# A linear-attention and snake-MLP kernel: the unused matmuls of its head made 512 columns wide

## The chip, the cores and the metric

The kernel runs on one core of one Trainium2 chip. The metric is the device time of one execution in microseconds (us). Three runs of the kernel before are shown, and a fourth execution was recorded by the hardware profiler.

## The reference, cut to what matters

Two layers follow each other. The first is causal linear attention with a decay per head, over 4 batches, 8 heads, 768 positions and a head width of 64. The second is a wide layer on the 3072 tokens by 512 features that come out.

```python
# attention, per block of 64 positions
intra = (qb @ kb.T * Dmask) @ vb
inter = (qb * lam_pow) @ kv_state
out[:, :, sl] = intra + inter
kv_state = lam_block * kv_state + (kb * rev_pow).T @ vb
# wide layer: 512 -> 2048 -> 512
h = x @ w_in
s = np.sin(alpha * h)
g = h + s * s / (alpha + 1e-09)
return g @ w_out
```

## The kernel before, in words

**Tiles.** Attention works on 24 blocks of 128 tokens. For each, q and k are scaled by powers of the decay (DVE or GpSimd, L462 to L492), transposed so that the head width lies on partitions (TensorE, L534, L560 and L511 for most of the early blocks, a DMA for the rest), and multiplied to scores (L612). DVE multiplies the scores by a mask (L623). Scores times v (L759, L716) and queries times the running state (L779, L694, L707) give the output of the block, which is copied to `xT`. The state itself is k times v, summed in PSUM (L648, L656) and copied to `Zd` or `Zc`. The wide layer takes chunks of 512 tokens. `unit_A` and `unit_A2` (L822, L856) make one or two slices of 128 hidden features: four matmuls each, then a sine on ScalarE, a square on ScalarE or GpSimd, and the sum on DVE. `unit_B` (L887) and `unit_P` (L975) make the second product.

**Head.** The first four blocks are loaded together. SyncE issues in this order: the decays, q in two halves, four loads of k, four loads of v, two loads `ws` of the first quarter of `w_in` (cast to `w1` by DVE at L384). GpSimd issues the loads of the other quarters of `w1` and of `w2` behind its casts of v (L486); ScalarE casts one of the four loads of v, in its own order ahead of the copies of the state (L666). TensorE's first state product (L648) needs two casts of v, both from GpSimd.

**Order.** No scheduler decides the order. `_Plan.ORDER` lists for each engine the numbers of its operations in the order in which it issues them; a semaphore wait is put where an operation depends on another engine. An engine issues strictly in this order, so an operation that waits holds back all behind it. In TensorE's list a pair like `(42,112)` isn't an operation. It is 42 unused matmuls of 112 columns, made by `spin` from a constant tile `idle` (which is part of `Xs`, set to 1.0 by DVE at L410) into PSUM bank 0. Their result is overwritten. They depend on nothing but `idle`, and nothing waits for them; they are recorded under L1134. Each has its own weight load, which is an instruction of its own.

TensorE's list begins as follows, with the meaning of the numbers:

```text
(42,112)  39: transpose of alpha (L444)
(30,128)  57: transposes of q (L534)    (11,128)  55: L534   (1,128)  53: L534   (1,128)  59: L534
(8,128)   61: transposes of k (L560)    (1,512)   62: L560
(3,512)   65, 67: scores (L612)   69, 70: L560   (3,512)  73: L612
75: first state product (L648)    78: L612   80: L759   82: L648   85: L779   (2,512)   87: L648
```

Of the kernel before, what the change touches and what calls it, by code (L numbers as in the profile page):

```python
# [33 lines left out]
class _Plan:  # L34

    ORDER = {
        "PE": (
            (42,112), 39, (30,128), 57, (11,128), 55, (1,128), 53, (1,128), 59, (8,128), 61, (1,512), 62,
            (3,512), 65, 67, 69, 70, (3,512), 73, 75, 78, 80, 82, 85, (2,512), 87, 90, 91, 93, 124, 130, 140,
            136, 151, 155, 147, 144, 167, 163, 159, 230, 228, 175, 171, 229, 232, 231, 233, 183, 191, 187, 179,  # L40
            235, 206, 207, 234, 209, 236, 217, 215, 237, 241, 221, 245, 319, 226, 320, 249, 250, 272, 252, 258,
# [1204 lines left out]
```

## Time and profile before

| What | us |
|---|---|
| median of three runs | 210.94 (210.78 to 211.43) |
| profiled execution, its own time | 211.5 |
| span in its trace, first to last instruction | 209.8 |
| TensorE busy in the span | 203.5 |
| DVE, ScalarE, GpSimd busy | 160.3, 158.7, 126.9 |

The span is shorter than the profiled execution's own time by 1.7 us, which lie around it. In the lines of the profile PE is TensorE's matmuls, PEld its weight loads, DVE is VectorE, ACT is ScalarE, POOL is GpSimd and SP is SyncE; a q behind an engine's name (SPq) is its sequencer, issuing a DMA. L534 is line 534 of the kernel. A line of a list in order of time has the start, the length and what ran, with xN for N instructions merged; brackets hold the idle time before it and what ended that. Matmuls overlap, so the length of a group ends with the tail of its last matmul. A row of a table of stretches has the stretch, its length, then for PE, PEld, DVE, ACT and POOL the busy time and the number of instructions, then the granted clock, the busy share of the DMA engines and GB/s. A row of a DMA queue has packets, MB and the share of 16 engines' time; a row of DMA issues ends with the time from issue to landing.

### The profile page before, as it was taken

The numbers are of one execution on the slowest core, as the hardware profiler recorded it, in microseconds if no ns is written. First come the engines' busy times: TensorE is split into PE (matmuls) and PEld (weight loads), VectorE is DVE, ScalarE is ACT, GpSimd is POOL, SyncE is SP. The second block draws the span as 40 slices with busy tenths as digits, with TensorE's granted clock in tenths as the row PEclk, the third lists the DMA queues.
The fourth block names the chain that finished last, engine by engine and source line by source line (L and its number), as shares of the span: only waits on it lengthen the run. The fifth ranks groups of instructions, "written<-read, shape, count | busy, mean of one in ns | idle before, by whom it ended". The sixth has DMA issues, their size and how long they took to land.

```text
span 209.8 us, 4867 instructions
## 1 busy us (share of the span) xinstructions
PE 203.5 (97%) x1975; PEld 134.3 (64%) x1975; DVE 160.3 (76%) x266; ACT 158.7 (76%) x294; POOL 126.9 (60%) x130
## 2 busy tenths in 40 slices
PE   7979999999999999999998999999999999999995
PEld 6847444457677776555555667766667765666894
DVE  4884557563999866868899799889698699777643
ACT  4949995968998989999997887787963889568210
POOL 7075354994469578679885392944581957378300
DMA  4999999999998999999999920190000004000514
GB/s 141 310 318 232 206 213 237 246 229 256 220 264 205 227 245 230 223 233 196 246 271 228 213 53 0 33 271 2 3 0 3 0 23 179 3 0 0 200 40 163
DMA packets 78998, 33.35 MB, mean 159 GB/s; under 512 B 55408, under 2 KB 76160, under 8 KB 78976
## 3 DMA queue, kind: packets, MB, share of 16 engines
q1 hardware_dynamic: 73744, 27.14, 56.2%
q0 software_dynamic: 3696, 3.67, 10.5%
q10 hardware_dynamic: 1536, 2.24, 3.3%
q8 instruction: 15, 0.25, 0.5%
q14 instruction: 7, 0.06, 0.1%
HBM read 27.28 MB, written 6.29 MB: 160 GB/s over the span
## 4 chain that ended last, share of the span: by engine, by line
PE 83%; DVE 6%; DMA 3%; SPq 3%; ACT 2%; issue 1%
PE bank L822 27%; PE bank L975 22%; PE bank L887 13%; PE bank L856 10%; DMA v<-in_v_dram 3%; PE bank L716 3%; SPq L315 3%; PE bank L612 3%; DVE gT L839 2%; PE bank L694 1%; DVE Sm L623 1%; PE bank L511 1%; PE bank L656 1%; DVE w L930 1%; PE bank L534 1%; PE bank L707 1%
## 5 line engine op out<-in xcount | busy, mean ns | idle before, releaser
L822 PE MATMUL bank<-xT,w 128*128 128x512 bf16 x296 | 70.5, 379 | 0.0
L839 DVE SCALAR_TENSOR_TENSOR gT<-u,rinv,bank 128x512 bf16<-128x512 bf16 x74 | 53.6, 742 | 18.2 <-ACT u L836 12.5
L832 ACT ACTIVATE t<-bank,alpha 128x512 bf16<-128x512 f32 x74 | 50.0, 684 | 21.0 <-PE bank L822 20.5
L822 PEld LDWEIGHTS bank<-xT,w 128*128 128x128 bf16 x296 | 28.3, 98 | 28.4 <-DVE gT L839 0.4
L836 ACT ACTIVATE u<-t 128x512 bf16<-128x512 bf16 x59 | 36.5, 628 | 1.3
L837 POOL TENSOR_TENSOR u<-t 128x512 bf16<-128x512 bf16 x15 | 16.0, 1066 | 34.1 <-ACT t L832 30.5
L953 POOL TENSOR_TENSOR gT<-gT 128x512 bf16<-128x512 bf16 x24 | 27.8, 1172 | 11.2 <-DVE Xs L953 6.0
L623 DVE TENSOR_TENSOR Sm<-bank,mask 128x1024 bf16<-128x1024 f32 x24 | 29.1, 1218 | 4.3 <-PE bank L648 1.8
L887 PE MATMUL bank<-w,gT 128*128 128x512 bf16 x128 | 31.4, 380 | 0.0
L874 DVE SCALAR_TENSOR_TENSOR gT<-u,rinv,bank 128x256 bf16<-128x256 bf16 x44 | 18.8, 476 | 7.8 <-ACT u L870 6.1
L472 POOL TENSOR_TENSOR qk<-q,Lq 128x512 bf16<-128x512 f32 x20 | 21.2, 1075 | 2.8 <-DMA q<-in_q_dram 2.8
L856 PE MATMUL bank<-xT,w 128*128 128x256 bf16 x176 | 22.2, 273 | 0.0
L492 POOL TENSOR_TENSOR qk<-k,Lk 128x512 bf16<-128x512 f32 x20 | 20.9, 1053 | 0.6 <-DMA k<-in_k_dram 0.6
L866 ACT ACTIVATE t<-bank,alpha 128x256 bf16<-128x256 f32 x44 | 18.9, 476 | 2.0 <-PE bank L856 1.5
L887 PEld LDWEIGHTS bank<-w,gT 128*128 128x128 bf16 x128 | 11.7, 98 | 12.2
L856 PEld LDWEIGHTS bank<-xT,w 128*128 128x128 bf16 x176 | 16.4, 98 | 3.5 <-issue 0.3
L953 POOL TENSOR_TENSOR Xs<-gT 128x512 bf16<-128x512 bf16 x13 | 16.1, 1235 | 1.5 <-DVE gT L839 1.4
L975 PE MATMUL bank<-w,gT 128*128 128x256 bf16 (+1 forms) x136 | 16.3, 266 | 0.0
L975 PE MATMUL bank<-w,Xs 128*128 128x256 bf16 (+1 forms) x136 | 16.0, 267 | 0.1
L975 PE MATMUL bank<-ws,gT 128*128 128x256 bf16 x128 | 15.8, 273 | 0.0
L975 PEld LDWEIGHTS bank<-w,gT 128*128 128x128 bf16 x136 | 12.6, 98 | 3.2
L975 PEld LDWEIGHTS bank<-w,Xs 128*128 128x128 bf16 x136 | 12.4, 98 | 2.8 <-DVE osb L1021 0.3
(101 smaller groups left out, 276.0 us busy)
## 6 DMA issues: line engine op xcount, KB each, us to landing
q<-in_q_dram SPq DMA_DIRECT2D x12, 512.0 KB, 6.2
k<-in_k_dram SPq DMA_DIRECT2D x24, 256.0 KB, 5.5
v<-in_v_dram SPq DMA_DIRECT2D x24, 256.0 KB, 5.4
out_dram<-osb SPq DMA_DIRECT2D x14, 256.0 KB, 2.5
w<-in_moe_w_out_dram POOLq DMA_DIRECT2D x4, 512.0 KB, 11.4
w<-in_moe_w_in_dram POOLq DMA_DIRECT2D x3, 512.0 KB, 9.0
ws<-in_moe_w_in_dram SPq DMA_DIRECT2D x2, 512.0 KB, 7.5
out_dram<-osb ACTq DMA_DIRECT2D x8, 128.0 KB, 4.0
```

What stands on the lines that cost most here:

```text
L472: lambda e, a=a: e.tensor_tensor(qk2[:, j:j + 2, 4 * a:4 * a + 4, :], q32[:, jq, 4 * a:4 * a + 4, :, :].rearrange("p h t d -> p t h d"), b ...
L492: lambda e: e.tensor_tensor(qk2[:, j, H:2 * H, :], block32(k32, jl), lk, ALU.mult), 1.05,
L623: op("DVE", lambda e: e.tensor_tensor(Sm[js][:, :, :], banks[:, 512 * b0:512 * b0 + 1024].rearrange("p (c i) -> p c i", i=128), bass.AP(ma ...
L822: ins = e.matmul(ps[hb][:, c0:c1], w1[:, kc, 128 * m:128 * (m + 1)], xT[x][:, kc, c0:c1], start=(kc == 0 and c0 == lo), stop=(kc == NKC - ...
L832: op("ACT", lambda e: e.activation(t16[ju][:, w], ps[hb][:, w], ACTF.Sin, scale=alpha[:, m:m + 1]), 0.69 if hi - lo == TCH else 0.475, [ba ...
L836: lambda e: (e.activation(u16[ju][:, w], t16[ju][:, w], ACTF.Square) if e is nc.scalar else e.tensor_tensor(u16[ju][:, w], t16[ju][:, w], ...
L839: op("DVE", lambda e: e.scalar_tensor_tensor(out=gT[g][:, m, w], in0=u16[ju][:, w], scalar=rinv[:, m:m + 1], in1=ps[hb][:, w], op0=ALU.mul ...
L856: ins = e.matmul(ps[hb][:, 256 * i:256 * i + 256], w1[:, kc, 128 * (m + i):128 * (m + i + 1)], xT[x][:, kc, lo:lo + 256], start=(kc == 0 a ...
L866: op("ACT", lambda e, i=i: e.activation(t16[ju][:, 256 * i:256 * i + 256], ps[hb][:, 256 * i:256 * i + 256], ACTF.Sin, scale=alpha[:, m + ...
L887: ins = e.matmul(ps[ob][:, w], gT[g][:, m, 128 * s4:128 * (s4 + 1)], w2[:, m, w], start=(m == 0), stop=(m == NM - 1),)
L953: e.tensor_tensor(dst, in0, in1, alu), 0, rd, wr))
L975: ins = e.matmul(ps[ob][:, lo + d0:lo + d1], lhs, rhs[:, d0:d1], start=first and p == 0, stop=(p == NM // 2 - 1), skip_group_check=True)
```

## The change

The first six pairs of TensorE's list are changed. Up to operation 61, the unused matmuls are all 512 columns wide; the two single ones between 55, 53 and 59 are gone. The pairs after 61 stay as they were. Counted up to 61, there were 93 unused matmuls and are 21. Nothing else differs, and the other engines issue the same instructions in the same order.

```diff
     ORDER = {
         "PE": (
-            (42,112), 39, (30,128), 57, (11,128), 55, (1,128), 53, (1,128), 59, (8,128), 61, (1,512), 62,
+            (9,512), 39, (7,512), 57, (3,512), 55, 53, 59, (2,512), 61, (1,512), 62,
             (3,512), 65, 67, 69, 70, (3,512), 73, 75, 78, 80, 82, 85, (2,512), 87, 90, 91, 93, 124, 130, 140,
```

## The prediction

> **What bounds the kernel now.** I read the page first, for the engine that sets the end.
>
> ```profile
> span 209.8 us, 4867 instructions
> ...
> PE 203.5 (97%) x1975; PEld 134.3 (64%) x1975; DVE 160.3 (76%) x266; ACT 158.7 (76%) x294; POOL 126.9 (60%) x130
> ...
> q8 instruction: 15, 0.25, 0.5%
> ...
> PE 83%; DVE 6%; DMA 3%; SPq 3%; ACT 2%; issue 1%
> ```
>
> TensorE is busy 97% of the span and holds 83% of the chain that ended last. So a shift of the moment when its dense work begins reaches the end. What the chain holds besides TensorE lies partly in the head, so the second view is the chain of waits cut to the first 20 us (start, length, what).
>
> ```profile
> 4.14 1.43 SPq L315
> ...
> 5.61 1.17 SPq L315
> ...
> 6.82 0.76 SPq L315
> ...
> 7.63 6.83 DMA v<-in_v_dram
> 14.46 0.02 issue
> 14.49 0.62 ACT v L486
> 15.11 0.27 ACT Zd L666
> ```
>
> Until 14.46 us the chain is not on TensorE at all. It is SyncE handing out loads, then the third load of v, then ScalarE's cast of it. The third view is TensorE's own order of time (start, length of the group, count; in brackets the idle time before it and what ended it).
>
> ```profile
> 1.52 3.55 PE L1134 MATMUL bank<-Xs 128*128 128x112 bf16 x42 [1.52 <-DVE Xs L410]
> 5.00 0.23 PE L444 MATMUL bank<-identf,alphaT 16*128 16x16 f32 x1
> 5.16 1.85 PE L1134 MATMUL bank<-Xs 128*128 128x128 bf16 x30
> 7.20 0.40 PE L534 MATMUL bank<-ident,qk 128*128 128x128 bf16 x4 [0.18 <-DVE qk L462]
> 7.43 0.78 PE L1134 MATMUL bank<-Xs 128*128 128x128 bf16 x11
> ...
> 9.74 0.39 PE L560 MATMUL bank<-ident,qk 128*128 128x128 bf16 x4
> 9.97 0.81 PE L1134 MATMUL bank<-Xs 128*128 128x512 bf16 x3
> 10.80 0.64 PE L612 MATMUL bank<-qkT 64*64 64x128 bf16 x32
> ...
> 12.96 0.42 PE L612 MATMUL bank<-qkT 64*64 64x128 bf16 x16
> 14.29 0.62 PE L648 MATMUL bank<-v,qk 64*128 64x128 bf16 x8 [0.90 <-POOL v L486]
> ```
>
> The unused matmuls (L1134) fill the time up to real work. At 14.29 TensorE has stood idle 0.90 us for GpSimd's cast of v. Whatever happened before that is forgotten there, as long as TensorE is less than 0.90 us late.
>
> **Why v is late.** The loads of k and v are alike (256 KB), so their landings should be evenly spaced. Here are four answers on DMA, each for the window in which one issue starts (last k, then v's first three; the last number is us from issue to landing), and one on the queues between 10.45 and 11.70 us.
>
> ```profile
> k<-in_k_dram SPq DMA_DIRECT2D x1, 256.0 KB, 6.4
> ```
> ```profile
> v<-in_v_dram SPq DMA_DIRECT2D x1, 256.0 KB, 5.8
> ```
> ```profile
> v<-in_v_dram SPq DMA_DIRECT2D x1, 256.0 KB, 6.7
> ```
> ```profile
> v<-in_v_dram SPq DMA_DIRECT2D x1, 256.0 KB, 6.8
> ```
> ```profile
> q8 instruction: 1, 0.02, 5.9%
> ```
>
> With the issue times of the chain (4.14, 5.61, 6.82, 7.63) the landings are 10.5, 11.4, 13.5 and 14.4 us: steps of 0.9, then 2.1, then 0.9. About 1.2 us were lost once, between the first and the second v. In that very stretch the instruction queue q8 read one packet of 0.02 MB, and it took 5.9% of 16 engines' 1.25 us, that is 1.18 us of one engine. A load has landed only when every engine has delivered its part. One engine held for 1.2 us therefore explains the step: all later loads on it stay late.
>
> Whose instructions are these? q8 read 15 packets, 0.25 MB; TensorE ran 1975 matmuls and as many weight loads, which is 263 of its instructions and 17 KB to a packet, 63 bytes each. No other engine has so many. The row of the stretches counts TensorE's instructions before the first read.
>
> ```profile
> 0.00:10.45 10.45, 8.74 (x122) 8.07 (x122) 6.69 (x17) 7.39 (x16) 3.88 (x16) 1.00 0.83 225
> 10.45:17.65 7.20, 5.91 (x138) 3.72 (x137) 5.89 (x7) 4.44 (x10) 5.64 (x8) 1.00 1.18 306
> ```
>
> The first read comes after 244 instructions. The second comes 275 later: the same q8 row answers for 17.65 to 18.90 us, and none for the time between. That is roughly every 256, by place in the program and not by time.
>
> [...]
>
> **The change part by part.**
>
> *Columns.* Up to the first transposes of q (L534) the fill goes from 42 x 112 + 30 x 128 = 8544 columns to 9 x 512 + 7 x 512 = 8192.
>
> ```profile
> L1134 PE MATMUL bank<-Xs 128*128 128x112 bf16 x24 | 2.4, 301 | 0.0
> ```
> ```profile
> 1.68 2.63 PE L1134 MATMUL bank<-Xs 128*128 128x112 bf16 x26
> ```
> ```profile
> 4.42 0.65 PE L1134 MATMUL bank<-Xs 128*128 128x112 bf16 x10
> ```
>
> The first 26 start (2.63 - 0.30) / 25 = 93 ns apart, 0.83 ns a column. The ten from 4.42 on take 0.65 us, with some 0.2 of tail 49 ns apiece. So the array runs at half rate until about 4.3 us and fully after, though the page shows a granted clock of 1.00 throughout. At full rate three 512-wide ones take 0.81 us and nine in the dense part 2.11 (row below): six more in 1.30, 216 ns each. A cold 512-wide one isn't in this trace: by columns 512 x 0.83 = 427 ns; at least 216 (full rate), at most about 635 (427 plus the 0.21 us by which 301 exceeds 93, if nothing overlapped). I take 427, the same stream. The first block then holds 2.78 us / 0.83 = 3340 cold columns; the rest is 1270 columns at 0.42 ns where it was 1360 in pieces of 112 at 49 ns: 0.53 in place of 0.60 us. The second takes 7 x 0.216 = 1.51 us against 30 x 0.056 = 1.68. TensorE waits 0.25 us longer for the transposes at 7.20, which DVE releases. Behind them 3 x 216 = 0.65 us stand for 11 x 56 = 0.61 (+0.03), the two single ones go, 2 x 216 stand for 8 x 56 (-0.02). The transposes at 9.74 and the scores at 10.80 come 0.07 us earlier. By itself this is worth nothing: the 0.90 us wait covers it. With 635 ns the first block would end at 5.4 to 5.6, and the wait at 7.20 still covers that.
>
> *Instructions.* 93 unused matmuls become 21: 72 matmuls with 72 weight loads go, 144 instructions. The first read now comes 144 instructions further on. Behind 10.45 us stand 32 + 8 + 3 + 16 + 8 = 67 matmuls up to the end of L648; 72 reaches five into the third group of scores. These wait for the second mask product on DVE:
>
> ```profile
> 11.27 3.49 DVE L623 TENSOR_TENSOR Sm<-bank,mask 128x1024 bf16<-128x1024 f32 x3 [0.41 <-PE bank L612]
> 13.61 0.62 POOL L486 CAST v<-v 128x512 bf16<-128x512 f32 x1 [1.31 <-DMA v<-in_v_dram]
> ```
>
> Two of three in 3.49 us end near 13.6. Even a read asked for 30 instructions ahead stands behind L612 at 12.9. Undelayed, the second v lands near 12.3 and the third near 13.2. So the read leaves v's way.
>
> *What is late next.* GpSimd's cast can end 1.2 us sooner, TensorE can start L648 0.90 + 0.07 sooner (a little more, as groups overlap), ScalarE's cast 1.26 sooner. That gives 1.0 to 1.1. Behind it stand loads that do not move:
>
> ```profile
> w<-in_moe_w_in_dram POOLq DMA_DIRECT2D x1, 512.0 KB, 7.4
> ```
> ```profile
> 14.17 0.95 POOL L315 DMA_DIRECT2D w<-in_moe_w_in_dram  x1
> ```
> ```profile
> 20.90 2.11 PE L822 MATMUL bank<-xT,w 128*128 128x512 bf16 x9
> ```
> ```profile
> 36.24 2.04 POOL L472 TENSOR_TENSOR qk<-q,Lq 128x512 bf16<-128x512 f32 x2 [0.67 <-DMA q<-in_q_dram]
> 39.69 0.61 PE L534 MATMUL bank<-ident,qk 128*128 128x128 bf16 x8
> 16.89 0.79 DVE L384 CAST w<-ws 128x1024 bf16<-128x1024 f32 x1 [0.36 <-DMA ws<-in_moe_w_in_dram]
> ```
>
> The second quarter of w1 lands at 14.17 + 7.4 = 21.6. Its first user is the ninth of those matmuls, at 20.90 + 8 x 0.216 = 22.63: 1.0 us of slack. The cast of ws ends at 17.68 for L856 at 18.99: 1.3 (the moved read holds one engine during ws, as the old one's lag did). q for block 4 is ready at 38.28 for 39.69: 1.4. So **about 1.0 us** passes, and from there TensorE is the bound. The profiled execution took 211.5 us (span 209.8 and 1.7 around it), so it would take 210.5. The median of the runs shown is 0.56 lower, 210.94; minus 1.0 it is 209.9. Bounds of the unknown: 0 (v not held up by the read), 1.3 (nothing late next).
>
> **The rivals.** 0.3% (0.63 us) is about what a measurement of this kernel tells from no change.
>
> - *The read doesn't cause v's step* (a packet of another load does): v lands as before, the 0.07 us vanish in the 0.90. 210.9. For it: no row names the engine that was late. Against it: one step in a regular series, of the read's own length, at its time.
> - *The full rate comes later.* Each 0.1 us by which TensorE is late at L648 now costs 0.1, since the idle 0.90 is used up. If the rate rose only at 7.7, the second block would start at 5.6, run 2.1 us cold and end at 8.2: 1.0 late, and the gain is gone, 210.9. [...]
> - *The rise counts weight loads* (slower). Before it came 30 of them. The wide fill makes a load only every 427 ns: 9 + 1 + 7 until 8.6 us, 4 transposes, 3, 4, and the thirty-first at 11.0. The last transposes then come 2.4 us later than at 9.74, the scores near 13.2, the next group, behind its mask product, near 15.4, and L648 near 15.7: 1.4 later than 14.29. 212.3. It decides from a rise later than 7.7. For it: only narrow fill is seen to raise the rate. Against it: the dense 512-wide part holds the full rate with one load per 216 ns.
>
> **How the numbers follow.** Forecast 0.70; read not the cause 0.11; rise near 7.7, 0.08; rise by loads 0.11. Predicted time 209.9. Forecast's own range 209.4 to 210.4 (0.6 to 1.3 us gained, 0.2 of scatter). The range goes up to 211.2, which takes in most of the two cases without change; the slow case is left out. Faster 0.70, same 0.19, slower 0.11.
>
> **What would show it.** Right: about 144 fewer TensorE instructions before the first read, which starts after 12.6 us; even steps of 0.9 us through all v landings; ScalarE's cast of v near 13.2 and L648 near 13.3; the first L856 near 18.0. Wrong: a v landing at 14.4 with the read elsewhere (then it wasn't the read); half rate after 5 us (then the clock decides); a new idle of TensorE at L822 or L534 (then a later load took the gain).

## The result, and the profile after

| | before | changed |
|---|---|---|
| runs, us | 211.43, 210.78, 210.94, 210.87 | 213.69, 222.39, 217.09, 213.91 |
| median, us | 210.91 | 215.5 |
| profiled execution, its span, us | 211.5, 209.8 | 213.69, 211.9 |

The change made the kernel slower where I forecast a gain of 1.0 us. The ratio is 1.0133, interval 1.0102 to 1.0163; here and below a ratio leaves out runs more than 1.5% above the fastest of their kernel, here those of 222.39 and 217.09 us (part 4 of the experiments is on these). First the page of the changed kernel.

```profile
span 211.9 us, 4697 instructions
...
PE 202.8 (96%) x1877; PEld 131.5 (62%) x1903; DVE 160.4 (76%) x266; ACT 158.8 (75%) x294; POOL 127.5 (60%) x130
...
PE 77%; DVE 12%; ACT 6%; issue 3%; POOL 1%; ACTq 0%
```

The chain that ended last now holds 3% of "issue", about 6 us in which an engine waited for nothing that the profile shows. TensorE's order of time says where the largest piece lies.

```profile
1.52 4.02 PE L1134 MATMUL bank<-Xs 128*128 128x512 bf16 x9 [1.52 <-DVE Xs L410]
5.47 0.28 PE L444 MATMUL bank<-identf,alphaT 16*128 16x16 f32 x1
5.69 1.73 PE L1134 MATMUL bank<-Xs 128*128 128x512 bf16 x7
7.26 0.39 PE L534 MATMUL bank<-ident,qk 128*128 128x128 bf16 x4
...
13.28 0.62 PE L648 MATMUL bank<-v,qk 64*128 64x128 bf16 x8
...
17.34 0.28 PE L779 MATMUL bank<-qkT,Zd 128*128 128x128 bf16 x2
20.05 0.80 PE L779 MATMUL bank<-qkT,Zd 128*128 128x128 bf16 x6 [2.44 <-issue]
20.65 3.01 PE L856 MATMUL bank<-xT,w 128*128 128x256 bf16 x16
```

From L648 to 17.3 us it went as forecast. L648 starts at 13.28 instead of 14.29, and it no longer waits for GpSimd's cast. The third load of v took 5.6 us from issue to landing, 6.8 before:

```profile
v<-in_v_dram SPq DMA_DIRECT2D x1, 256.0 KB, 5.6
```

Then TensorE stops in the middle of eight equal matmuls (L779), after the second. The instruction queue has no packet between 11.7 and 17.3 us; for 17.35 to 18.75 it has this:

```profile
q8 instruction: 1, 0.02, 5.8%
```

5.8% of 16 engines' 1.40 us is 1.30 us of one engine: the moved read. TensorE goes on 1.3 us after the end of that window. The table of stretches shows the rest.

```profile
0.00:12.93 12.93, 11.04 (x92) 5.41 (x94) 8.83 (x20) 8.50 (x18) 6.02 (x19) 1.00 0.88 238
...
0.00:17.62 17.62, 15.53 (x219) 8.68 (x222) 12.38 (x23) 12.99 (x27) 10.61 (x25) 1.00 0.96 258
```
```profile
18.00:20.00 2.00, 0.00 (x0) 0.00 (x0) 0.00 (x0) 0.00 (x0) 0.00 (x0) 0.87 1.22 200
20.00:22.00 2.00, 1.95 (x13) 1.57 (x13) 1.02 (x2) 1.03 (x2) 0.00 (x0) 0.50 1.23 206
22.00:24.00 2.00, 1.95 (x13) 1.44 (x13) 0.00 (x0) 1.37 (x3) 0.00 (x0) 0.78 1.24 205
```

All five engines stand still for two microseconds; only the DMA goes on. Then the granted clock falls to 0.50, which is half rate: the shares 0.87, 0.50 and 0.78 stand for 0.13 x 2 / 0.5 = 0.52, then 2.00, then 0.22 x 2 / 0.5 = 0.88 us, 3.4 in all; the first half microsecond of it falls into the stop (the trace's record of the clock has 0.50 from 19.49 to 22.90 us). So:

| start of | before | changed | difference |
|---|---|---|---|
| L648, first | 14.29 | 13.28 | -1.0 |
| L856, first | 18.99 | 20.65 | +1.7: -1.0, then 2.65 from the stop (17.40 to 20.05) |
| L822, first | 20.90 | 23.71 | +2.8: 1.15 more for the 16 matmuls of L856 at half rate |
| L534, next block | 39.69 | 42.28 | +2.6 |
| end of the span | 209.8 | 211.9 | +2.1 |

The 0.7 us that come back on the way to the end I did not follow up. Two questions were left for the chip: why TensorE stopped there, and what makes single runs of 217 and 222 us.

The **theory**: TensorE's instructions come in blocks, one to each read. How many a block holds is an estimate from the trace of before: 15 reads for 3950 matmuls and weight loads make 263 to a read, and between the starts of the first read (244 issued) and the last (3761 by 198.26 us) lie 14 blocks of 251. I take 257, the middle. TensorE's last instruction before the stop is about number 441 (219 matmuls and 222 weight loads in the row to 17.62; the page lists 26 matmuls fewer than weight loads, so a few records are missing; the traces below that lack none put it at 443). One block less than 443 is 186 (180 with 263, 192 with 251); the changed kernel has issued 186 by 12.93 us (92 and 94), 180 by 11.95 and 192 by 12.94. The kernel before had done so by 8.30, as its rows of the same table show:

```profile
0.00:8.30 8.30, 6.59 (x93) 6.31 (x93) 4.59 (x13) 5.55 (x12) 3.88 (x16) 1.00 0.73 208
```
```profile
0.00:15.30 15.30, 12.52 (x221) 10.41 (x225) 10.60 (x21) 9.58 (x20) 7.17 (x21) 1.00 0.93 254
```

If the next read is asked for when a block has been run through, it was asked for at 8.3 us and ran at 10.5 before; it was asked for at 12.9 and ran at 17.4 after. The request itself is not in the trace. Before, number 443 was due at about 15.3 (446 by 15.30) and the read over at 11.7; now it was due at 17.4 and the read not begun. The **rivals**: width itself (512 columns disturb loads or clock), a fixed lag of the read, or something else at L779.

### The profile page after: what moved, and what is told of

It reads as the page before. It is cut to its first block, busy times and chain, and to the rows that moved or that the text cites. A ratio compares the mean times of both kernels' runs of the same rounds, so it can differ in the third digit from the quotient of the medians.

```text
span 211.9 us, 4697 instructions
## 1 busy us (share of the span) xinstructions
PE 202.8 (96%) x1877; PEld 131.5 (62%) x1903; DVE 160.4 (76%) x266; ACT 158.8 (75%) x294; POOL 127.5 (60%) x130
## 4 chain that ended last, share of the span: by engine, by line
PE 77%; DVE 12%; ACT 6%; issue 3%; POOL 1%; ACTq 0%
PE bank L822 23%; PE bank L975 18%; PE bank L887 11%; PE bank L856 10%; DVE gT L839 5%; PE bank L1134 4%; PE bank L612 3%; ACT t L832 3%; PE bank L716 2%; DVE Sm L623 2%; ACT u L836 2%; DVE w L930 2%; PE bank L534 1%; POOL u L837 1%; PE bank L648 1%
## 5 line engine op out<-in xcount | busy, mean ns | idle before, releaser
L822 PE MATMUL bank<-xT,w 128*128 128x512 bf16 x280 | 67.8, 379 | 1.2 <-issue 0.3
L822 PEld LDWEIGHTS bank<-xT,w 128*128 128x128 bf16 x296 | 28.3, 98 | 28.4 <-DVE gT L839 0.4
L837 POOL TENSOR_TENSOR u<-t 128x512 bf16<-128x512 bf16 x15 | 16.0, 1066 | 38.3 <-ACT t L832 34.8
L887 PE MATMUL bank<-w,gT 128*128 128x512 bf16 x120 | 29.9, 379 | 0.6 <-issue 0.3
L856 PE MATMUL bank<-xT,w 128*128 128x256 bf16 x176 | 23.2, 282 | 0.0
L856 PEld LDWEIGHTS bank<-xT,w 128*128 128x128 bf16 x176 | 17.1, 101 | 3.7
L887 PEld LDWEIGHTS bank<-w,gT 128*128 128x128 bf16 x128 | 11.7, 98 | 12.2
L871 POOL TENSOR_TENSOR u<-t 128x512 bf16<-128x512 bf16 x7 | 7.3, 1041 | 13.3 <-ACT t L866 13.2
L975 PEld LDWEIGHTS bank<-w,gT 128*128 128x128 bf16 x136 | 12.6, 98 | 3.2
```

Source lines behind the costliest of these rows:

```text
L822: ins = e.matmul(ps[hb][:, c0:c1], w1[:, kc, 128 * m:128 * (m + 1)], xT[x][:, kc, c0:c1], start=(kc == 0 and c0 == lo), stop=(kc == NKC - ...
L856: ins = e.matmul(ps[hb][:, 256 * i:256 * i + 256], w1[:, kc, 128 * (m + i):128 * (m + i + 1)], xT[x][:, kc, lo:lo + 256], start=(kc == 0 a ...
L887: ins = e.matmul(ps[ob][:, w], gT[g][:, m, 128 * s4:128 * (s4 + 1)], w2[:, m, w], start=(m == 0), stop=(m == NM - 1),)
L975: ins = e.matmul(ps[ob][:, lo + d0:lo + d1], lhs, rhs[:, d0:d1], start=first and p == 0, stop=(p == NM // 2 - 1), skip_group_check=True)
```

## The experiments

In all, before was run on the same chip; its medians there were 210.9 to 211.3 us.

### 1. The width, or the number of instructions

`e3` keeps wide matmuls and pads with 72 of 16 columns, so that only 16 instructions go:

```diff
-(9,512), 39, (7,512), 57,
+(4,512), (72,16), 39, (4,512), 57,
```

> Wide fill (4, 4, 3 and 2 of 512 columns) with 72 matmuls of 16 columns added behind the first four, so that only 16 instructions are missing against before. Theory A: the read is asked for at 8.3 to 8.7 us as before, begins at 10.5 to 11.4, v is late again by about 1.2 us for at least one load, no stall: 210.5 to 211.2. Theory B: half rate again after 17 us, 213 or more.

Measured: 211.37 us (210.59 to 212.13), ratio 1.0016, 0.9997 to 1.0035, 0.2 us above what theory A forecast. The read is back in its old place; for 10.45 to 11.70 us the queue has the row of before:

```profile
q8 instruction: 1, 0.02, 5.9%
```

The third v took 6.8 to 6.9 us again, L648 started at 14.36, and no stop came. Width alone makes no stop and no gain.

`e5` keeps the number of matmuls of the change and halves their width:

```diff
-(9,512), 39, (7,512), 57, (3,512), 55, 53, 59, (2,512), 61,
+(14,256), 39, (4,256), 57, (2,256), 55, 53, 59, (1,256), 61,
```

> The change with every one of its 21 unused matmuls half as wide: 14, 4, 2 and 1 of 256 columns. As many instructions as the change (144 fewer than before), half the columns, so TensorE idles before the first transposes. Theory A (the number of instructions decides): TensorE stops after its 221st matmul, at about 17.4 us, for 2 to 3 us; 213 to 216. Theory B (the width decides): no stop or a shorter one, 212.5 or less.

Measured: 217.34 us (212.37, 217.0, 217.68, 222.23; no ratio). TensorE stopped after 221 matmuls and 222 weight loads, from 18.43 to 20.63, a stop of 2.2 us as theory A had it, 1 us later. So the number of instructions sets the stop. With the shorter fill the array fell back to half rate for a while: three matmuls of 512 columns took 1.49 us at 10.21 (0.81 in the change), and L648 was late (14.09). The profile was of the run of 222.23 us and showed what part 4 follows.

### 2. One block of the fill undone

`e1` puts `(42,112)` back in the first place (78 instructions fewer than before), `e2` `(30,128)` in the second (98 fewer).

> The change with its first block of unused matmuls put back to 42 of 112 columns; the others stay 512 wide. 78 instructions fewer than before in place of 144. Theory A (the place of the instruction read decides: TensorE must have the next 16 KB before it has used up what it holds): the read is asked for near 10.9 us, begins near 13.4 (two to three us later, as 8.3 to 10.5 before), after the last v; TensorE would run out only near 17, so there is no stall, L648 starts near 13.3 and the time is 209.9, 1.0 below before. Theory A2 (a read is served only when all loads issued so far are through, near 17.4): a stall stays, of 2 to 3 us near 17, time 213 to 215. Theory B (wide matmuls in themselves lower the clock or start the work late): half rate after 17 us again, 212 or more, as three of the four wide blocks are left.

> The change with its second block put back to 30 of 128 columns. 98 instructions fewer than before. Theory A: asked for near 11.1 us, begins near 13.4, no stall, 209.9 to 210.2. Theory A2: a stall of over 2 us near 17.2, 213 to 215. Theory B: as with the change, 213 or more, since the wide cold block is still there.

Measured: `e1` 210.72 us, ratio 0.9989 (0.9967 to 1.0012); `e2` 210.75, ratio 0.9982 (0.9962 to 1.0002). Both win time at L648 (13.65, 14.03) and lose it in a stop. No theory had that: A had no stop, A2 one of 2 us or more, B a half rate. Of `e1`, the table of stretches and TensorE's order of time:

```profile
0.00:17.36 17.36, 15.57 (x221) 10.89 (x222) 12.61 (x23) 12.28 (x26) 10.44 (x25) 1.00 0.95 259
```
```profile
17.13 0.24 PE L759 MATMUL bank<-Sm,v 64*64 64x128 bf16 x1
18.36 0.64 PE L759 MATMUL bank<-Sm,v 64*64 64x128 bf16 x31 [1.00 <-issue]
```

Here the stop falls after the first of 32 matmuls of another line, and in `e2` after 11 of these 32 (0.74 us, from 17.9 on), each time at 221 matmuls and 222 weight loads, 443 in all. So the place is set by the count, not by the line. The read ran at 15.72 in `e1` and 16.09 in `e2`, though number 186 was issued by about 11.4 and 12.0. After these stops, of 1.00 and 0.74 us, the clock stayed at full rate (1.00 over both runs). The load that lands late has changed, too. It is now the second `ws`, issued at 10.5 us; from issue to landing it took 7.9 us in `e1`, 7.8 in `e2` and 6.7 in the change (the first and the last for the window from 10.5 to 11.3 us):

```profile
ws<-in_moe_w_in_dram SPq DMA_DIRECT2D x1, 512.0 KB, 7.9
```
```profile
ws<-in_moe_w_in_dram SPq DMA_DIRECT2D x1, 512.0 KB, 6.7
```

So in `e1` and `e2` the read held up the second `ws` by about 1.2 us, as it held up the second v before.

### 3. What stands ahead of the read

`e4` to `e8` ask what makes the lag of 2.2 us (before) into 4.5 (change). `e4` moves the load of k for block 4 behind the load of q on SyncE. `e6` holds the two loads `ws` back until the first two loads of v have landed; `e7` is this with the first block `(42,112)` put back; `e8` is this alone, in the kernel before.

```diff
-    ("ws", lo), 1.47, f"ws{lo}", lat=0.65, runs=32,
+    ("ws", lo), 1.47, f"ws{lo}", lat=0.65, runs=32, after=[last["v32", lo // 256]],
```

> The change as it is, but the load of k for block 4, which SyncE issues at 12.6 us, is moved behind the load of q for block 4 (issued after 20 us); 144 instructions fewer, wide fill. Theory A with A2 for the wait (the read stands behind the loads that are queued): without that load in front the read begins near 16.5 in place of 17.4, TensorE stands still until about 19.1 in place of 20.05, and the time falls by about 0.9 to 212.8. Theory A with a fixed delay of the read: begins at 17.4 again, 213.7. Theory B: no difference, 213.7.

Measured: 216.65 us, ratio 1.026 (1.0236 to 1.0284). The read came at 16.10 instead of 17.39 and the first stop shrank to 0.93 us, without half rate. But the late k held GpSimd's list up for 7.8 us, and TensorE waited for it at 39.7. Its whole time says nothing on the theory; the place of its read speaks against a fixed lag, and TensorE went on at 18.76, where theory A with A2 had 19.1.

> The change as it is, with fewer loads queued when the read is asked for: SyncE issues the first load of ws only when the first v has landed (near 11.4 us) and the second when the second v has (near 12.3). Theory C (the read stands behind the loads already queued on its DMA engine): the read begins near 15.2 in place of 17.4, TensorE starts again near 18.0 in place of 20.05, no half rate after; 210.0 to 211. Theory D (the read takes a fixed 4 to 5 us in this part, whatever is queued): 17.4 again, 213.5 to 215.

Measured: 213.2 us (210.86 to 220.87), ratio 1.0049 (1.0018 to 1.0079), 1.009 by the medians of all runs. A miss: the read still came at 17.0 and the stop stayed (TensorE's order of time):

```profile
19.89 0.78 PE L779 MATMUL bank<-qkT,Zd 128*128 128x128 bf16 x6 [2.21 <-issue]
```

SyncE had issued both `ws` by 12.8 us and k at 12.8 to 13.3, mostly ahead of number 186 (12.95). The edit came too early to help this request.

> First block put back to 42 of 112 columns (78 instructions fewer than before), and the loads of ws gated as in the run beside it. Theory C: the read, asked for near 10.9 us, begins near 13.4, behind the last v; TensorE has its next instructions before the 221st matmul, no stop near 17; the 1.0 us from the earlier v stays: 209.7 to 210.1. Theory D: read near 15.7, a stop of 1.2 us, 210.7.

Measured: 210.46 us (209.96 to 211.27), ratio **0.9961** (0.9943 to 0.9979), below the kernel before. Number 186 is issued by about 11.3 us, ahead of the first `ws` (11.39). The read runs at 13.01 instead of 15.72 in `e1`; the queue's row for 13.0 to 14.2 us and TensorE's order of time:

```profile
q8 instruction: 1, 0.02, 6.0%
```
```profile
16.95 0.64 PE L759 MATMUL bank<-Sm,v 64*64 64x128 bf16 x32
17.52 0.74 PE L779 MATMUL bank<-qkT,Zd 128*128 128x128 bf16 x8
18.10 2.07 PE L856 MATMUL bank<-xT,w 128*128 128x256 bf16 x16
20.01 2.21 PE L822 MATMUL bank<-xT,w 128*128 128x512 bf16 x9
```

No stop, and L822 starts 0.9 us sooner than before's 20.90. That is most of the gain that I forecast, got with a read that stands neither in v's way nor past its due time. Of the runs' time it is 0.8 us by the ratio, and 0.4 in `e10` (part 4), which has the same head.

> The kernel before with only the loads of ws gated, as a control. The read is asked for near 8.3 us, ahead of the gated loads: it begins at 10.5 as before, v stays late, 210.7 to 211.1 under every theory; more would mean that the gating costs time of its own.

Measured: 211.16 us, ratio 0.9987 (0.997 to 1.0005); read at 10.95, v late and L648 at 14.31 as before. So the gated loads alone gain nothing, nor does the block alone (`e1`); `e7` gains by the read's place.

### 4. The runs of 217 and 222 us

`e9` moves two sums of w on VectorE (L930, operations 430 and 429) to a place where VectorE and GpSimd are idle; `e11` does it to before, `e10` to `e7`; `e12` is the changed kernel again.

```diff
-... 158, 162, 166, 430, 178, 174, 429, 186, 190, 208, 194, 210, 182, 216, 222, 227, 432, 259,
+... 158, 162, 166, 178, 174, 186, 190, 208, 194, 210, 182, 216, 222, 227, 430, 429, 432, 259,
```

> The change with two of VectorE's operations (numbers 430 and 429, the sums of w at L930) moved behind the cast at L726 that ends at 51.6 us in the changed kernel, where VectorE is idle until 54.3 and GpSimd until 55.5. Nothing before 100 us reads these sums. If the runs of the changed kernel at 217 and 222 us come from these sums waiting beside GpSimd's run of 34.6 to 44 us (7.50 us at 36.63 in the run of 222 us with 256 columns, 0.68 elsewhere), all runs of this kernel lie at 213 to 214.5, none above 216, and its stop at 17.4 to 20.0 is as in the changed kernel. If those runs have another cause, some of its runs lie at 217 or more as well.

> The changed kernel itself again, on the chip of the run with the sums moved, to hold the spread of the two against each other. If the sums cause the long runs, some of its runs lie at 217 or more and the rest at 213 to 214.5; if they do not, this kernel and the one with the sums moved spread alike.

Measured: `e12` 214.27 us with runs of 217.49 and 222.47 among six, ratio 1.015 (1.013 to 1.0169); `e9` 213.62, 212.05 to 213.97 in six, ratio 1.011 (1.0082 to 1.0138). Of ten runs of the change, on two occasions, four lay at 217 or above; of six of `e9`, none. Chance alone would put all four among the ten about one time in nine, so the count says little, and the trace has to say the rest. The profile of `e12` was of the run of 222.47 us. Its VectorE and GpSimd in order of time, and its view of waits:

```profile
36.72 7.49 DVE L930 TENSOR_TENSOR Ta<-w 128x1024 bf16<-128x1024 bf16 x1
```
```profile
36.48 2.04 POOL L472 TENSOR_TENSOR qk<-q,Lq 128x512 bf16<-128x512 f32 x2
38.48 1.03 POOL L492 TENSOR_TENSOR qk<-k,Lk 128x512 bf16<-128x512 f32 x1
39.48 4.18 POOL L930 TENSOR_TENSOR ws<-w 128x1024 bf16<-128x1024 bf16 x2
```
```profile
PE bank L822 <- DVE gT L839: 4.7, 1, 4.7
```

A sum that takes 0.68 us elsewhere takes 7.49 and ends 0.55 after GpSimd's unbroken run (43.66). Behind it on VectorE stands the product that TensorE's L822 needs, so TensorE idles 4.7 us and then works at a clock of 0.50 from 44 to 48. In the profiled run of 213.69 us the same sum started 1.26 us earlier and met a gap in GpSimd's work, from 35.67 to 35.94:

```profile
35.46 0.77 DVE L930 TENSOR_TENSOR Ta<-w 128x1024 bf16<-128x1024 bf16 x1
```
```profile
35.94 2.19 POOL L472 TENSOR_TENSOR qk<-q,Lq 128x512 bf16<-128x512 f32 x2 [0.27 <-DMA q<-in_q_dram]
```

Before, it ran at 32.86, ahead of GpSimd's work. The stop moves TensorE and VectorE by 2.8 us, while GpSimd's run hangs mostly on landings that did not move; the sum thus falls on its edge, on the one side of it or the other. In these two profiled runs the half rate behind the stop decided the side. In the run of 222.47 us it lasted twice as long: by the rows below, worked out as for the change, 6.8 us instead of 3.4.

```profile
18.00:20.00 2.00, 0.23 (x3) 0.23 (x3) 0.00 (x0) 0.00 (x0) 0.00 (x0) 0.74 1.24 203
20.00:22.00 2.00, 2.00 (x14) 1.54 (x12) 1.02 (x2) 1.04 (x2) 0.00 (x0) 0.50 1.25 209
22.00:24.00 2.00, 1.98 (x10) 1.32 (x10) 0.16 (x1) 1.47 (x3) 0.00 (x0) 0.50 1.24 206
24.00:26.00 2.00, 1.80 (x5) 0.69 (x5) 0.71 (x2) 1.12 (x3) 0.00 (x0) 0.56 1.23 208
```

TensorE was 1.27 us later there when it left L822 for L648 (29.18 for 27.91). In `e5`'s run of 222.23 us the sum started at 36.63 and took 7.50. No run near 217 us of the change was profiled, so for those the cause is not shown. Why the sum takes 7.49 us for 0.68 beside GpSimd's work no trace shows; that the one holds the other up is my reading of the two lists above.

> The kernel before with the same two sums moved, as the measure of the move alone. There both sums ran in 0.7 us, so both theories expect 210.6 to 211.2 us, the time of the kernel before, and as little spread.

> The kernel with the first block of 42 put back and the loads of w's first part behind v (210.46 us, its sum at L930 took 3.65 us at 34.62), with the same two sums moved. If that sum held TensorE up, this is 209 to 210.2 us; if the wait was covered, 210.4 as there.

Measured: `e11` 210.82 us, ratio 0.9991 (0.9977 to 1.0006); `e10` 210.64, ratio 0.9979 (0.9964 to 0.9994). Neither gains by the move beyond the noise; `e7`'s sum of 3.65 us was covered.

### 5. The whole change, with a read that comes in time

`e13` holds `ws` back until the third v has landed (`after=[last["v32", 2]]`), so that of SyncE's loads this request, too, should have only the last v ahead of it. `e14` adds the moved sums.

> The whole change, with the two loads of ws issued only after the third load of v has landed (13.24 us), and with them the load of k behind them on SyncE; in the run where they waited for the first two loads of v all three were issued by 13.3 us, around the request of the instruction read at 12.93. If the read waits for what was issued ahead of it, it now has only the last load of v before it (14.13): it starts at 14.1 to 15.0 in place of 17.39, TensorE stops for 0.3 us at most after its 221st matmul, there is no half rate, L822 starts at 19.9 to 20.3 (20.90 before, 23.71 in the change), and the run takes 209.5 to 210.8 us. If the lag of 4.5 us does not come from these loads, the read starts near 17.4 again, L822 at 23.7, and the run takes 213 to 214 us.

> The same, with the two sums at L930 (430 and 429) moved as in the run of the change with the sums later. Head as there. If the stop goes, 209.3 to 210.6 us and no run above 212; if it stays, 213 to 214 us.

Measured: `e13` 216.53 us, ratio 1.0244 (1.0202 to 1.0286); `e14` 215.67, ratio 1.0209 (1.0169 to 1.025). The times missed, the mechanism held: the read ran at 14.33 in `e13` and 14.45 in `e14`, 1.0 and 1.5 us after number 186, and the stop is gone. `e13`'s queue for 14.3 to 16.4 us, then its TensorE and VectorE in order of time:

```profile
q8 instruction: 1, 0.02, 5.9%
```
```profile
17.77 0.74 PE L779 MATMUL bank<-qkT,Zd 128*128 128x128 bf16 x8
19.37 1.92 PE L856 MATMUL bank<-xT,w 128*128 128x256 bf16 x16 [0.86 <-DVE w L384]
25.07 1.49 PE L822 MATMUL bank<-xT,w 128*128 128x512 bf16 x3 [3.77 <-DVE gT L874]
```
```profile
23.91 0.69 DVE L384 CAST w<-ws 128x1024 bf16<-128x1024 f32 x1 [4.24 <-DMA ws<-in_moe_w_in_dram]
```

A new wait took its place. The second `ws` landed at 23.89 (17.19 in the change), with loads of w under way that GpSimd had issued from 12.97 on. `e15` and `e16` (the moved sums added) put GpSimd's cast of the last v ahead of its loads of w:

```diff
-... 50, 47, 48, 102, 103, 52, 105, 106, 104,
+... 50, 47, 48, 52, 102, 103, 105, 106, 104,
```

> The change with ws after the third load of v (as before this run) and GpSimd's first two loads of w behind its cast of the last v, so from 14.7 us in place of 12.95 and behind ws, which SyncE issues at 13.28 to 14.2. The read starts at 14.1 to 15.0 and TensorE does not stop after its 221st matmul. ws should land by 17 and 18.7 us, the second in place of 23.89: L856 at 17.6 to 18.3, L822 at 19.9 to 20.5, and the run 209.5 to 210.8 us, below the kernel before. If the change costs time at a place other than this stop, the head is as said and the run still takes over 212 us.

> The same with the two sums at L930 moved. Head as there; 209.3 to 210.5 us if the stop was the cost of the change, over 212 if another place was.

Measured: `e15` 212.8 us (one run 217.54), ratio 1.008 (1.0057 to 1.0104); `e16` 212.71 (one run 216.24), ratio 1.0063 (1.0034 to 1.0092). Reads at 13.84 and 15.78, no stop in `e15` and 0.1 us of one in `e16`, clock full up to L822. The forecast of 209.3 to 210.8 missed again: in the profiled runs `ws` still landed late (23.51 and 20.05), so that the order against w was not, or not alone, what held it up, and in `e16` L822 then waited for w (chain of waits):

```profile
15.16 9.24 DMA w<-in_moe_w_in_dram
```

By their own condition these two say that the stop is not the only cost once other loads are moved; they do not say what the change would take with nothing but the stop removed. That, in the whole change, was not reached: in the ways tried, the read got ahead only of loads that have no time to give.

## Why the prediction was wrong, step by step

**What bounds the kernel; why v is late: right.** A head that is 1.0 us sooner at L648 reaches L822 when nothing else comes between (`e7`: 0.8 us at L648, 13.47 for 14.29, and 0.9 at L822). And the read is what held v up: with it back (`e3`, `e8`) v is late, with it gone (change, `e1`, `e7`) v is even. The trace's records of landings show that it was one part of the load: of the 16 parts of the second v, 15 had landed by 12.28 us before and the last at 13.56, and GpSimd's cast began at 13.61; in the change all 16 had landed by 12.34.

**Columns: right in price, late in rate, and covered.** Nine cold 512-wide matmuls fill 1.52 to 5.47 us, 0.42 apart but for the tail of the last (427 ns was taken). Seven from 5.69 to 7.26 are 0.224 apart, full rate. So the rate rose near 5.8, not 4.3, and long before a thirtieth weight load: the rival that counts loads is refuted, and the rival of a later rise happened without cost, since L534 began at 7.26 (7.20 before) and the wait for v covered it. That was luck. The rise moves from run to run, whatever the width: in `e8`, whose fill is that of before, the first block took 4.10 us in place of 3.55.

```profile
1.52 4.10 PE L1134 MATMUL bank<-Xs 128*128 128x112 bf16 x42 [1.52 <-DVE Xs L410]
```

And with the fill of the change L534 began at 7.09 in `e9` and at 7.88 in `e13`, where L648 came at 13.72.

**Instructions: the failing step.** "So the read leaves v's way" asked where the read would be harmless to v, and not by when TensorE needs what it reads; the read's cost to TensorE was put at nothing. I took the read's start as fixed by the count, 244 instructions on, and put it "after 12.6". It came at 17.39, with 441 instructions recorded. Before, TensorE has no gap at the read of 10.5, but that read had a slack of 3.6 us behind it (over at 11.7, number 443 due at 15.3). I took the missing gap as proof that a read costs TensorE nothing. But, by the theory, the request moved by 4.6 us (8.3 to 12.9) and the due time only by 2.1 (15.3 to 17.4). TensorE goes on about 2.6 us after a read's start (17.39 to 20.05, in `e1` 15.72 to 18.36). Even with the old lag of 2.2, then, 12.9 + 2.2 + 2.6 = 17.7 stands against 17.4: no slack was left. The lag of 4.5 made the stop 2.65 us. None of the signs of being wrong that I listed names a stop of TensorE for its own instructions; the half rate "after 5 us" came, but as its consequence.

**What is late next: incomplete.** The list named loads that others wait for and left out this one. The loads that it does name were in time as far as 17 us. It left out, too, VectorE's place beside GpSimd.

**What a crossing costs.** From one block of instructions to the next TensorE lost 2.65 us in the change and 1.23 in `e1` (17.13 to 18.36), and v 1.2 before; in `e7` TensorE lost nothing. So the crossing was hidden for TensorE before and in `e7`, and not in the change. With 2.44 us of idle time went some 3.4 us at 0.50, with some 2.2 us in the long run of `e12` some 6.8, and with 1.00 us in `e1` none; what decides on the half rate and its length, these runs do not show.

The sum with the missing terms: -1.0 + 2.65 + 1.15 = +2.8 us at L822, against +2.81 measured.

**Open.** When the read is asked for, and behind which loads it stands. Counted from number 186 the lags are 1 to 2.2 us when `ws` was issued with it or after it (`e7`, `e13` to `e16`), 3.2 with `ws` but not k ahead (`e4`) and 4 to 4.5 with both (change, `e1`, `e2`, `e6`). That fits a queue, but not one that is served strictly by the time of issue and asked at number 186: in `e1` and `e2` the read went ahead of the second `ws`, and before ahead of the second v, which SyncE had issued at 6.82, before number 186 at 8.3. Either the read is asked for earlier, or it overtakes loads; no trace shows the request. Some of the lag is no queue: in `e13` the DMA engines moved nothing from about 13.5 to 14.3 us, and the read still came 1.0 us after number 186. Nor is it clear why TensorE goes on only some 1.4 us after the read's end. The longest runs of `e15` and `e16` were not traced to a cause shown by itself.

## What to carry to other kernels

Count an engine's instructions, not only their time: an edit that removes or adds some can move the reads of instructions behind it (here the first one from 10.50 us to 15.72 with 78 fewer and to 17.39 with 144 fewer), against the loads and against the moment when the engine runs dry. For each read look up three times in the trace: when the block before was run through, when the packet ran, and when its first instruction was due; a read that shows no gap may have much slack or none. Where loads were issued early and in numbers, the read came late here (4 to 4.5 us after number 186, 1 to 2.2 us where they were not ahead of it), so a load that is not yet needed is better issued after the read's request, but only if it has time to give.

## What the runs showed that I had not expected

One read of instructions, some 17 KB by the prediction's count, stopped all five engines for two microseconds, and the idle time was paid a second time at half rate. One VectorE instruction took 6.8 us more beside GpSimd's (7.49 for 0.68 us), which, with a half rate that lasted twice as long, turned 2.8 us of delay into 11 in a single run (222.47 against 211.04, the median of before on that chip). And the moment at which the full rate comes in the head moved from run to run with the same fill: the first 42 matmuls took 3.55 or 4.10 us.
